# A causal convolution and a maxout feed-forward layer on one core: convolution groups of five blocks, an early exp table, and tiles at multiples of 256 bytes

## The chip, the core and the metric

The kernel runs on one core of a Trainium2 chip. The metric is the device time of one execution in microseconds (us). The kernel before takes 454.34 us, the median of three runs (454.12 to 455.48). Engines are named as the profile names them: PE is TensorE (matmuls; PEld its weight loads), DVE is VectorE, ACT is ScalarE, POOL is GpSimd, SP is the engine that issues most DMAs.

## The reference

The input `x` is 8 x 4160 x 192 in float32. The first layer is a causal convolution of 7 taps along the sequence; each of 8 heads has its own 7 weights (a softmax) for its 24 channels. The second layer is a maxout of three products with 768 columns, followed by a product back to 192 columns.

```python
w = np.exp(weight - np.max(weight, axis=-1, keepdims=True))
w = w / (np.sum(w, axis=-1, keepdims=True) + 1e-09)
x_pad = np.concatenate([np.zeros((B, K - 1, D)), x], axis=1)
y = np.einsum('hk,bskhg->bshg', w, unfold(x_pad)).reshape(B * S, D)
h = np.maximum(np.maximum(y @ w1, y @ w2), y @ w3)
out = h @ w_out
```

## The kernel before

**Blocks.** The 33280 rows are cut into 65 blocks of 512 tokens. Blocks 0 to 3 go through a dense convolution (`conv_dense`); block 4 stands alone, blocks 5 to 12 go in pairs, and blocks 13 to 64 in groups of four (`pairs`, lines 172 to 175; `place(t)` gives a block's group, its position in it and the group's size). The blocks of a group are convolved together.

**The way of a block.** SP loads its rows of x in float32 into a tile `xf`, one of three that take turns in the steady part (`load_x`). POOL casts it to float16 into its place in the group's tile `x16` (`cast_x`, line 194). TensorE convolves (`conv`, line 357): the 8 heads times 4 token strips times 2 halves are 64 matmuls for a group, each 39 rows by 32 columns of weights from the tile `band`, which holds the softmax weights as a banded matrix; the moving side has 48 columns for each block of the group, so 192 for a group of four. Groups of four are convolved in two halves of 4 heads (32 matmuls), in two successive blocks. A half writes four PSUM tiles G: two from the pool `psw`, one from `psp`, one from `psq` (`WPWQ`). `evac` (line 397) casts them to float16 in `ys`, two on ACT (those of `psw`) and two on DVE (those of `psp` and `psq`). `turn` (line 411) has SP transpose `ys` into the tile `yp` by DMA, two blocks at a time, and `double` (line 420) has POOL copy `yp` across the two halves of the partitions.

**The feed-forward layer.** For block t and column tile j (6 of 128 columns), `l1` forms two products lp and lq in PSUM, with weights that are differences with w3 (`wd`); `top` takes the relu of lp on ACT (line 490) and the larger of it and lq on DVE (line 491), which gives `h`. What the differences leave out is added back in the second product by the small matrices `m16`. `st2` forms the output product po of block t-1 (line 567), ACT copies one half, DVE adds the other (lines 574, 575), SP stores the result.

**The order.** All instructions stand in the program's own order (`manual_schedule`). PE is used as two halves of 64 rows, two lanes, that run side by side; `mm` queues matmuls by lane, `emit` gives them out so that the lanes' columns stay level, and `meet` empties both lanes. A convolution needs the whole array, so `meet` stands before it. In the loop over t (line 747) a block whose entry in `convs_at` names a group (`late`) does that group's convolution after column tile 1. For a group that begins at u these are blocks u-4 and u-3; `turn(u)` follows in u-3, and the third and fourth blocks' `turn` in u-2. The tables `casts` and `loads` say which block's cast and load is issued in which block t.

**PSUM buffers.** `psp` and `psq` have two buffers each. lp and lq of successive column tiles alternate between them, and a convolution takes one of each in between: lp and lq of column tile 3 of a late block go into the buffers that the two DVE casts of G have just emptied.

**The start.** ACT's queue loads the conv weights `wk`; the softmax on ACT and DVE (lines 265 to 274), 38 small matmuls that spread it (line 283) and casts on ACT and DVE (line 287) make `band`. Beside it SP loads x and the weights of the second layer into `ws` and `w3s`, POOL and DVE form `wd` from them (line 302), and PE runs matmuls on zeros (`keep_warm`, line 252) between its first tasks. ACT also writes zeros into parts of later `xf` tiles (line 137). The first product of block 0 with weights is `l1_dense` (line 526).

Of the kernel before, what the change touches and what calls it, by code (L numbers as in the profile page):

```python
# [10 lines left out]
FP32 = mybir.dt.float32  # L11
FP16 = mybir.dt.float16
AXX = mybir.AxisListType.X
# [15 lines left out]
def kernel(  # L29
# [71 lines left out]
    x16q = ctx.enter_context(tc.tile_pool(name="x16q", bufs=2))  # L101
    ysp = ctx.enter_context(tc.tile_pool(name="ysp", bufs=2))
    ydp = ctx.enter_context(tc.tile_pool(name="ydp", bufs=4))
    ypp = ctx.enter_context(tc.tile_pool(name="ypp", bufs=4))
    rp = ctx.enter_context(tc.tile_pool(name="rp", bufs=4))
    hp = ctx.enter_context(tc.tile_pool(name="hp", bufs=2))
    tp = ctx.enter_context(tc.tile_pool(name="tp", bufs=2))
# [3 lines left out]
    psq = ctx.enter_context(tc.tile_pool(name="psq", bufs=2, space=bass.MemoryType.PSUM))  # L111
    psw = ctx.enter_context(tc.tile_pool(name="psw", bufs=4, space=bass.MemoryType.PSUM))

    QUADS = 13
    assert (NB - QUADS) % 4 == 0
    xin, xbuf, XBUF, loaded = {}, [], 7, set()

    def get_x(t):
# [52 lines left out]

    pairs = {NDENSE: (NDENSE, 0, 1)}
    for t in range(NDENSE + 1, NB):
        u = (t - NDENSE - 1) % 2 if t < QUADS else (t - QUADS) % 4
        pairs[t] = (t - u, u, 2 if t < QUADS else 4)

    def place(t):
        return pairs.get(t, (t, 0, 0))
# [3 lines left out]
    def cast_x(t):  # L182
        if not 0 <= t < NB:
            return
        xf, p0, _ = xin.pop(t)
        t0, u, nu = place(t)
        if u == 0:
            pool = x16q if nu == 4 else x16p
            x16s[t0] = pool.tile([P, NHEAD, 4, nu, 2, GRP], FP16, tag="x16", name=f"x16_{t0}")
        if p0:  # L190
            nc.gpsimd.memset(xf[0:p0, 0, :], 0.0)
        K = HALF + KR
        for r in range(2):
            nc.gpsimd.tensor_copy(out=x16s[t0][0:K, :, :, u, r, :].rearrange("p h j c -> p j h c"),  # L194
                                  in_=xf[0:K, 4 * r:4 * r + 4, :].rearrange("p j (h c) -> p j h c", c=GRP))
# [18 lines left out]

    ws = const.tile([P, NC, DFF], FP32)
    w3s = const.tile([P, 2, DFF], FP32)
    PW = 2 * P

    def load_wa(f):
# [4 lines left out]
        for st, lo, n, wsrc in ((w3s, 0, 1, moe_w3), (ws, 0, 2, moe_w1), (ws, HALF, 2, moe_w2)):  # L226
            nc.sync.dma_start(out=st[lo:lo + HALF, n, f], in_=wsrc[P:D, f])

    wk = const.tile([NHEAD, KW], FP32)
    nc.scalar.dma_start(out=wk[:], in_=weight)  # L230
    wos = const.tile([P, NJ, D], FP32)
    load_x(0)
    load_wa(slice(0, PW))
# [21 lines left out]

    line = const.tile([NHEAD, WIN + 31], FP16)
    nc.vector.memset(line[:], 0.0)
    for v in range(2):  # L260
        nc.vector.memset(xz[0][v][:], 0.0)
    band = const.tile([P, NHEAD, BAND_W], FP16)
    nc.vector.memset(band[:], 0.0)
    keep_warm(5, psp, "p")
    wexp = const.tile([NHEAD, KW + 1], FP32)
    nc.vector.memset(wexp[:], 1e-9)
    wneg = const.tile([NHEAD, 1], FP32)
    nc.vector.reduce_max(out=wneg[:], in_=wk[:], axis=AXX, negate=True)
    nc.scalar.activation(out=wexp[:, 0:KW], in_=wk[:], func=AF.Exp, bias=wneg[:])  # L269
    wrec = const.tile([NHEAD, 1], FP32)  # L270
    nc.vector.reduce_sum(out=wrec[:], in_=wexp[:], axis=AXX)
    nc.vector.reciprocal(out=wrec[:], in_=wrec[:])
    zero_x(4)
# [21 lines left out]
    wd = const.tile([P, NC + 1, DFF], FP16)  # L295
    w3t = const.tile([P, NJ, 2 * P], FP16)
    wo = const.tile([P, NJ, D], FP16)
    m16 = const.tile([P, 3, D], FP16)

    def make_wd(n, j0, j1, eng=nc.vector):  # L300
        f = slice(P * j0, P * j1)
# [99 lines left out]
    def turn(t, vs=(0,)):  # L401


        nu = place(t)[2]
        for v in vs:
            n = min(nu, 2)
            yp = ypp.tile([P, 2, 2, n, NC, P], FP16, tag="yp", name=f"yp_{t + v}")
            for u in range(n):
                dense[t + v + u] = yp
            for i in range(2):  # L410
                nc.sync.dma_start_transpose(out=yp[:, 0, i, :, :, :].rearrange("p u k n -> p (u k) n"),
                                            in_=slots[t][:, i, v:v + n, :, :].rearrange("p u r d -> p (u r d)"))
# [10 lines left out]
    def spot(t, i, c, r):  # L423

        _, u, nu = place(t)
        u, nu = u % 2, min(nu, 2)
        f = NC * (r % 2) + c
        return (((f % 2 != i) * 2 + r // 2) * nu + u) * NC + f // 2

# [299 lines left out]

    convs_at = {2: 4, 3: 5, 4: 7}  # L730
    convs_at.update({t - 3: t for t in range(9, QUADS, 2)})
    convs_at.update({t - 4 + i: t for t in range(QUADS, NB, 4) for i in range(2)})
    casts = {4: 9}
    for t in range(5, NB):
        casts[t] = min(NB - 1, casts[t - 1] + (2 if t in (6, 7, 8) else 1))
    loads = {t: min(NB - 1, casts.get(t + 1, 0) + (t < 7 or t > 9)) for t in range(4, NB)}
    loads.update({2: 9, 3: 10})

    def load_on(t):
        for v in range(loads[t - 1] + 1, loads[t] + 1):  # L740
            if v not in loaded:
                load_x(v)
# [4 lines left out]
    for t in range(2, NB):  # L747
        u = convs_at.get(t, NB)
        late = t > 2 and u < NB
        if t in (3, 4):  # L750
            double(t + 1)
        if t > 3:
            for v in range(casts.get(t - 1, 8) + 1, casts[t] + 1):
                cast_x(v)
        l1(t, 0)
        if t == 2:
            first_rest()
        elif t == 3:
            cast_x(8)
            nc.gpsimd.tensor_copy(out=m16[0:HALF, 2, :], in_=m16[HALF:P, 0, :])  # L760
            nc.gpsimd.tensor_copy(out=m16[HALF:P, 2, :], in_=m16[HALF:P, 1, :])
        if t > 3 and not late:
            op(lambda t=t: (store(t - 2, 0, 4, (nc.sync,)),
                            turn(t + 2, (2,)) if place(t + 2)[1:] == (0, 4) else None, load_on(t)))
        else:
            op(lambda t=t: store(t - 2, 0, 4, (nc.sync,)))
        cuts = ROOM if late else EVEN
        st2(t - 1, (cuts[0], cuts[0]))
        for j in range(1, NJ):
            l1(t, j)  # L770
            if late and j == 1:
                st2(t - 1, (cuts[0] + OWN + AHEAD, cuts[0] + OWN))
                meet()
                quad, second = u >= QUADS, u < QUADS or t == u - 3
                conv(u, WPWQ, range(4 * second, 4 * second + 4) if quad else range(NHEAD))
                for i in (0, 2):
                    evac(u, i)
                for i in (1, 3):
                    evac(u, i, nc.vector.tensor_copy)
                if second:  # L780
                    turn(u)
                load_on(t)
            if t == 2 and j == 1:
                meet()
                conv_dense(3, (ACT, DVE))
                zero_x(1, NQ, NR, nc.vector)
                cross(3, GP)
                load_x(8)
                cast_x(6)
            elif t == 2 and j == 3:  # L790
                meet()
                conv(u, WW)
                evac(u, 0)
                evac(u, 1, nc.vector.tensor_copy)
                turn(4)
                load_x(9)
                cast_x(7)
            st2(t - 1, (cuts[j], cuts[j]))
            if j == 1 and t > 4 and t + 2 in pairs and pairs[t + 2][1] % 2 == 0:
                double(t + 2)  # L800
            if t == NB - 1 and j == 3:
                op(lambda: store(NB - 2, 0, 2, (nc.sync,)))
        if t == NB - 1:
            op(lambda: store(NB - 2, 2, 4, (nc.sync,)))
# [29 lines left out]
```

## Time and profile before

| What | us |
|---|---|
| median of three runs | 454.34 |
| the profiled execution | 454.51 |
| its span (first to last instruction) | 452.7 |
| PE busy | 446.8 |
| DVE busy | 356.5 |
| ACT busy | 320.0 |
| POOL busy | 202.9 |
| idle time of POOL ended by x loads / by transposes | 93.0 / 75.9 |
| mean of a DVE cast of G, 128x384 | 0.550 |
| mean of an ACT cast of G, 128x384 | 0.482 |

The profile is of one execution. Its page gives each engine's busy time; "the chain that ended last" follows the work back from the last instruction, at each step to what released it, so it tells which engine's work sets the time in each stretch. "The waits" list, for an engine, whom it sat idle for. The timeline shows rows of equal instructions with the first one's start, their time, and in brackets the idle time ahead of them. A busy engine that is not on the chain can become faster without any effect on the end.

### The profile page before, as it was taken

The numbers are of one execution on the slowest core, as the hardware profiler recorded it, in microseconds if no ns is written. First come the engines' busy times: TensorE is split into PE (matmuls) and PEld (weight loads), VectorE is DVE, ScalarE is ACT, GpSimd is POOL, SyncE is SP. The second block draws the span as 40 slices with busy tenths as digits, with TensorE's granted clock in tenths as the row PEclk, the third lists the DMA queues.
The fourth block names the chain that finished last, engine by engine and source line by source line (L and its number), as shares of the span: only waits on it lengthen the run. The fifth ranks groups of instructions, "written<-read, shape, count | busy, mean of one in ns | idle before, by whom it ended". The sixth has DMA issues, their size and how long they took to land.

```text
span 452.7 us, 18493 instructions
## 1 busy us (share of the span) xinstructions
PE 446.8 (99%) x7702; PEld 412.6 (91%) x7702; DVE 356.5 (79%) x617; ACT 320.0 (71%) x604; POOL 202.9 (45%) x226
## 2 busy tenths in 40 slices
PE   7999999999999999999999999999999999999997
PEld 3569999999999999999999999999999999999996
DVE  7768778878878787887878788887878788787775
ACT  7767767767777676777767777776767777776664
POOL 2864836556454534645263464535346452505000
PEclk9999999999999999999999999999999999999999
DMA  7969997596875869587685949657594776535223
GB/s 205 231 178 166 199 205 195 146 206 180 169 180 147 168 129 207 138 176 185 118 190 141 210 117 184 177 136 186 133 206 124 178 189 118 117 89 104 59 72 106
DMA packets 127987, 72.03 MB, mean 159 GB/s; under 512 B 52064, under 2 KB 127711, under 8 KB 127903
## 3 DMA queue, kind: packets, MB, share of 16 engines
q1 hardware_dynamic: 127743, 70.75, 68.3%
q8 instruction: 60, 0.98, 1.0%
q14 instruction: 24, 0.20, 0.1%
q10 hardware_dynamic: 160, 0.10, 0.1%
HBM read 33.28 MB, written 25.56 MB: 130 GB/s over the span
## 4 chain that ended last, share of the span: by engine, by line
PE 97%; ACT 1%; DMA 0%; DVE 0%; issue 0%; ACTq 0%
PE po L567 36%; PE lq L503 31%; PE lp L503 22%; PE G L357 3%; PE lw L526 1%; PE lp L526 1%; PE D L378 1%; PE po L625 0%; PE po L598 0%; DMA wk<-in_weight_dram 0%; PE lq L526 0%; ACT xf L137 0%; ACT band L287 0%; ACT L269 0%; PE pm L337 0%; PE band L283 0%
## 5 line engine op out<-in xcount | busy, mean ns | idle before, releaser
L491 DVE TENSOR_TENSOR h<-r,lq 128x512 f16<-128x512 f16 x384 | 263.0, 686 | 85.1 <-ACT r L490 77.3
L567 PE MATMUL po<-wo,h 64*128 64x192 f16 x3024 | 329.8, 243 | 0.0
L490 ACT ACTIVATE r<-lp 128x512 f16<-128x512 f32 x384 | 229.0, 597 | 114.3 <-PE lp L503 100.8
L503 PE MATMUL lp<-yp,wd 64*128 64x512 f16 x1098 | 295.6, 376 | 0.0
L503 PE MATMUL lq<-yp,wd 64*128 64x512 f16 x1098 | 295.5, 376 | 0.0
L567 PEld LDWEIGHTS <-h 64*128 64x128 f16 x3024 | 240.9, 94 | 6.3 <-issue 4.1
L503 PEld LDWEIGHTS <-wd 64*128 64x128 f16 x2268 | 177.7, 94 | 10.6 <-issue 0.2
L194 POOL CAST x<-xf 103x768 f16<-103x768 f32 x122 | 97.5, 827 | 106.6 <-DMA xf<-in_x_dram 93.0
L567 PE MATMUL po<-m,yp 64*128 64x192 f16 x720 | 141.0, 243 | 0.0
L420 POOL COPY yp<-yp 64x1536 f16<-64x1536 f16 (+1 forms) x62 | 89.6, 1445 | 96.2 <-DMA yp<-ys 75.9
L575 DVE TENSOR_TENSOR o<-a,po 128x384 f32<-128x384 f32 x126 | 69.0, 547 | 0.0
L567 PEld LDWEIGHTS <-yp 64*128 64x128 f16 x720 | 66.3, 94 | 0.5
L574 ACT COPY a<-po 128x384 f32<-128x384 f32 x126 | 59.5, 472 | 0.0
L397 ACT CAST ys<-G 128x384 f16<-128x384 f32 x61 | 26.3, 482 | 9.5 <-PE G L357 9.4
L397 DVE CAST ys<-G 128x384 f16<-128x384 f32 x61 | 31.0, 550 | 0.0
L357 PE MATMUL G<-x,band 39*32 39x192 f16 (+2 forms) x1152 | 17.3, 234 | 0.0
L357 PEld LDWEIGHTS <-band 39*32 39x32 f16 x1152 | 10.7, 91 | 5.2 <-issue 4.7
L503 PE MATMUL lp<-yd,wd 64*128 64x512 f16 x36 | 9.7, 376 | 0.0
L503 PE MATMUL lq<-yd,wd 64*128 64x512 f16 x36 | 9.7, 376 | 0.0
L526 PEld LDWEIGHTS <-wd 128*128 128x128 f16 (+1 forms) x48 | 3.2, 98 | 5.7 <-issue 2.4
L211 POOL CAST xz<-xf 112x160 f16<-112x160 f32 (+2 forms) x15 | 4.1, 319 | 7.7 <-DMA xf<-in_x_dram 7.7
L378 PEld LDWEIGHTS <-xz 112*32 112x32 f16 x320 | 4.6, 107 | 2.7 <-issue 1.0
(74 smaller groups left out, 98.2 us busy)
## 6 DMA issues: line engine op xcount, KB each, us to landing
xf<-in_x_dram SPq DMA_DIRECT2D x113, 234.0 KB
out_dram<-o SPq DMA_DIRECT2D x62, 384.0 KB
xf<-in_x_dram SPq DMA_DIRECT2D x7, 204.8 KB
xf<-in_x_dram SPq DMA_DIRECT2D x3, 420.0 KB
ws<-in_moe_w_dram SPq DMA_DIRECT2D x8, 128.0 KB
yp<-ys SPq DMA_TRANSPOSE x62
out_dram<-o SPq DMA_DIRECT2D x5, 192.0 KB
wos<-in_moe_w_out_dram SPq DMA_DIRECT2D x1, 576.0 KB
```

What stands on the lines that cost most here:

```text
L194: nc.gpsimd.tensor_copy(out=x16s[t0][0:K, :, :, u, r, :].rearrange("p h j c -> p j h c"), in_=xf[0:K, 4 * r:4 * r + 4, :].rearrange("p j ( ...
L357: nc.tensor.matmul(G[2 * (k // per) + i][TOK * j:TOK * (j + 1), k % per, :], lhsT=band[row, h, HALF * i + LAP:HALF * i + KR], rhs=x16s[t0] ...
L378: nc.tensor.matmul(ps[32 * g:32 * g + 32, lo:hi], lhsT=xz[t][v][0:rlen, q, 32 * s:32 * s + 32], rhs=band[0:rlen, h, cc:cc + hi - lo], star ...
L397: copy(out=slots[t][:, i % 2, :, :, GRP * h0:GRP * (h0 + per)].rearrange("p u r (h c) -> p h (u r) c", c=GRP), in_=G[i][:].rearrange("p h ...
L420: nc.gpsimd.tensor_copy(out=yp[HALF * i:HALF * (i + 1), 1, :, :, :, :].rearrange("p i u k n -> p (i u k n)"), in_=yp[HALF * (1 - i):HALF * ...
L490: nc.scalar.activation(out=r[:], in_=ps[0][:], func=AF.Relu)
L491: nc.vector.tensor_max(out=hs[t][:, j, :], in0=r[:], in1=ps[1][:])
L503: nc.tensor.matmul(ps[i][:], lhsT=w_of(i, c, j), rhs=y_all(t, i, c), start=(n == 0), stop=(n == NC - 1))
L526: nc.tensor.matmul(open_ps[t, j, i][:], lhsT=a, rhs=b, start=(t, j, i) not in begun, stop=(t, j, i) in begun)
L567: nc.tensor.matmul(ps[b0, i][:, s % 2, :], lhsT=a, rhs=b, start=first, stop=last)
L574: nc.scalar.copy(out=a[:], in_=ps[s - 1, 0][:])
L575: nc.vector.tensor_add(out=outs[t][:, s - 1:s + 1, :], in0=a[:], in1=ps[s - 1, 1][:])
```

## The change

- **Groups.** Blocks 25 to 64 are convolved in 8 groups of five; blocks 13 to 24 stay in 3 groups of four. The matmuls of a group of five move 240 columns. `turn` takes the blocks of a group as two, two and one; the fifth block's transposes are issued in block u-1 after the store. From block 16 on every cast, and with it every load, comes one block earlier. The pool of `yp` gets a fifth buffer, `x16` and `ys` grow to the size of five.
- **Weights in a pool.** `ws` and `w3s` are no longer tiles of their own: they are views of one buffer of the pool of `x16`, which a later group uses again.
- **Exp table.** A one-element exp on a zero tile stands on ACT right after the issue of the load of `wk`, so the table of exp is loaded there. The maximum of `wk` and the real exp come before the memset of `band` in DVE's and ACT's order.
- **Addresses.** A filler tile and rounded sizes of the small tiles put every tile that a DMA reads or writes at a multiple of 256 bytes within its partition.

```diff
-    ypp = ctx.enter_context(tc.tile_pool(name="ypp", bufs=4))
+    ypp = ctx.enter_context(tc.tile_pool(name="ypp", bufs=5))
...
-    QUADS = 13
-    assert (NB - QUADS) % 4 == 0
+    QUADS, QUINTS = 13, 25
+    assert (QUINTS - QUADS) % 4 == 0 and (NB - QUINTS) % 5 == 0
+    LINE = 256
+    SMALL = LINE // 4
+    const.tile([P, LINE // 4], FP16, name="edge")
...
-        u = (t - NDENSE - 1) % 2 if t < QUADS else (t - QUADS) % 4
-        pairs[t] = (t - u, u, 2 if t < QUADS else 4)
+        first_, nu = (NDENSE + 1, 2) if t < QUADS else (QUADS, 4) if t < QUINTS else (QUINTS, 5)
+        u = (t - first_) % nu
+        pairs[t] = (t - u, u, nu)
...
-            pool = x16q if nu == 4 else x16p
-            x16s[t0] = pool.tile([P, NHEAD, 4, nu, 2, GRP], FP16, tag="x16", name=f"x16_{t0}")
+            pool = x16q if nu >= 4 else x16p
+            x16 = pool.tile([P, NHEAD * 4 * 2 * GRP * (5 if nu >= 4 else nu)], FP16, tag="x16", name=f"x16_{t0}")
+            x16s[t0] = x16[:, 0:NHEAD * 4 * 2 * GRP * nu].rearrange("p (h j u r c) -> p h j u r c", h=NHEAD, j=4, u=nu, r=2)
...
-    ws = const.tile([P, NC, DFF], FP32)
-    w3s = const.tile([P, 2, DFF], FP32)
+    wall = x16q.tile([P, NHEAD * 4 * 2 * GRP * 5], FP16, tag="x16", name="wall")
+    wall = wall[:].bitcast(FP32).rearrange("p (n f) -> p n f", f=DFF)
+    ws, w3s = wall[:, 0:NC, :], wall[:, NC:NC + 2, :]
...
-    wk = const.tile([NHEAD, KW], FP32)
+    wk = const.tile([NHEAD, SMALL], FP32, name="wk")[:, 0:KW]
     nc.scalar.dma_start(out=wk[:], in_=weight)
+    warm = const.tile([1, SMALL], FP32, name="warm")[:, 0:1]
+    nc.vector.memset(warm[:], 0.0)
+    nc.scalar.activation(out=warm[:], in_=warm[:], func=AF.Exp)
...
-    band = const.tile([P, NHEAD, BAND_W], FP16)
+    wexp = const.tile([NHEAD, SMALL], FP32, name="wexp")[:, 0:KW + 1]
+    nc.vector.memset(wexp[:], 1e-9)
+    wneg = const.tile([NHEAD, SMALL], FP32, name="wneg")[:, 0:1]
+    nc.vector.reduce_max(out=wneg[:], in_=wk[:], axis=AXX, negate=True)
+    nc.scalar.activation(out=wexp[:, 0:KW], in_=wk[:], func=AF.Exp, bias=wneg[:])
+    bands = const.tile([P, LINE // 2 * ceil(NHEAD * BAND_W * 2 / LINE)], FP16, name="band")
+    band = bands[:, 0:NHEAD * BAND_W].rearrange("p (h w) -> p h w", w=BAND_W)
     nc.vector.memset(band[:], 0.0)
     keep_warm(5, psp, "p")
-    wexp = const.tile([NHEAD, KW + 1], FP32)
-    nc.vector.memset(wexp[:], 1e-9)
-    wneg = const.tile([NHEAD, 1], FP32)
-    nc.vector.reduce_max(out=wneg[:], in_=wk[:], axis=AXX, negate=True)
-    nc.scalar.activation(out=wexp[:, 0:KW], in_=wk[:], func=AF.Exp, bias=wneg[:])
-    wrec = const.tile([NHEAD, 1], FP32)
+    wrec = const.tile([NHEAD, SMALL], FP32, name="wrec")[:, 0:1]
...
-            n = min(nu, 2)
+            n = min(nu - v, 2)
...
-    convs_at.update({t - 4 + i: t for t in range(QUADS, NB, 4) for i in range(2)})
+    convs_at.update({t - 4 + i: t for t in (*range(QUADS, QUINTS, 4), *range(QUINTS, NB, 5)) for i in range(2)})
...
-        casts[t] = min(NB - 1, casts[t - 1] + (2 if t in (6, 7, 8) else 1))
+        casts[t] = min(NB - 1, casts[t - 1] + (2 if t in (6, 7, 8, 16) else 1))
...
-                            turn(t + 2, (2,)) if place(t + 2)[1:] == (0, 4) else None, load_on(t)))
+                            turn(t + 2, (2,)) if place(t + 2)[1:] in ((0, 4), (0, 5)) else None,
+                            turn(t + 1, (4,)) if place(t + 1)[1:] == (0, 5) else None, load_on(t)))
```

## The prediction

> **What bounds the kernel now.** I read the busy times first, then the chain that ended last, then the waits of TensorE, and last two stretches of the timeline: the start, and one convolution in the steady part. The busy times, TensorE's part of the waits, and the chain in order of time (columns: start, duration, what):
>
> ```profile
> span 452.7 us, 18493 instructions
> PE 446.8 (99%) x7702; PEld 412.6 (91%) x7702; DVE 356.5 (79%) x617; ACT 320.0 (71%) x604; POOL 202.9 (45%) x226
> ...
> PE band L283 <- DVE line L274: 1.3, 1, 1.3
> PE idle L252 <- DVE idle L247: 1.2, 1, 1.2
> ...
> 0.75 1.69 DMA wk<-in_weight_dram
> 2.50 1.28 ACT L269
> 7.14 1.48 ACT xf L137
> 9.27 0.58 PE lp L526
> 104.87 0.45 PE G L357 x32
> 111.80 0.46 PE G L357 x32
> 131.44 0.45 PE G L357 x32
> ```
>
> From 9.27 us on the chain is TensorE alone, and TensorE waits for no one in the steady part. So only two things can move the end: TensorE's own work, and the chain ahead of 9.27. Nothing that POOL, SP or the DMAs gain counts, unless they become late. The three convolution lines give prices. From 104.87 to 111.80 lies one block with one half convolution, 6.93; from there to 131.44 lie three blocks with one, 19.64. So a plain block takes (19.64 - 6.93) / 2 = 6.355 and a half convolution adds 6.93 - 6.355 = 0.575. Two half convolutions serve a group of four.
>
> The same convolution at closer range, the timeline of VectorE and TensorE (an idle time before the row stands in brackets):
>
> ```profile
> 104.96 0.69 DVE L491 TENSOR_TENSOR h<-r,lq 128x512 f16<-128x512 f16 x1 [0.37 <-ACT r L490]
> 105.56 1.01 DVE L397 CAST ys<-G 128x384 f16<-128x384 f32 x2
> 106.83 0.69 DVE L491 TENSOR_TENSOR h<-r,lq 128x512 f16<-128x512 f16 x1 [0.25 <-ACT r L490]
> ...
> 106.33 0.38 PE L503 MATMUL lp<-yp,wd 64*128 64x512 f16 x1
> 106.67 0.38 PE L503 MATMUL lq<-yp,wd 64*128 64x512 f16 x1
> ```
>
> The convolution takes one of the two buffers of each of the pools psp and psq. The two VectorE casts empty them, and the lp and lq of column tile 3 are next in those buffers: in the built program both carry a wait for VectorE. The second cast ends at 105.56 + 1.01 = 106.57; lq starts at 106.67. A wait on VectorE takes about 0.05 from its end to TensorE's start (line's end 4.73, band's start 4.78), so the margin is about 0.05 us, the smallest that I find in the loop.
>
> **The change, part by part.**
>
> *Fewer, wider convolutions.* Blocks 25 to 64 are 10 groups of four before and 8 of five after: 20 half convolutions become 16. Without growth that is 4 x 0.575 = 2.30 saved.
>
> Each half convolution has 32 matmuls on 8 places of the array, four rounds; in the trace the rounds start 0.083 us apart, which for 192 columns is 80 ns of streaming at 512 columns in 0.213 us (the lp matmuls follow each other by 0.216) and 3 ns more. With 240 columns a round is 0.103. So 4 x 0.020 = 0.08 more for each, 16 x 0.08 = 1.28. If nothing waits, the part saves 2.30 - 1.28 = 1.02.
>
> The casts of G grow from 384 to 480 columns. VectorE's rows: 384 columns 0.550 (cast of G), 512 columns 0.692 (cast of D), which is 1.1 ns a column; from start to start 0.467 for 384 columns and 0.60 for 512. So 480 columns take 0.65, and the next can start after 0.567. The first starts where it does now, since it queues behind h of column tile 1 and not behind the convolution. So the second ends 0.10 + 0.10 = 0.20 later, at 106.77, and lets lq go at 106.82. TensorE is ready for it at 106.67 + 0.08, less 0.01 that it waits for the h of tile 1 now and will not: 106.74. That is a wait of about 0.08 where there is none, on the lane of lq. The lp lane goes on (its next matmul is due 0.09 after lq, 106.76 now), but both lanes must be drained before the next convolution, and in the trace the lq lane's last matmul ends no earlier than the other's. So the 0.08 is paid each time: 16 x (0.08 + 0.01 lost slack) = 1.3. I take +0.3 for the whole part (1.28 + 1.3 - 2.30). Its bounds: -1.0 with no wait, and +0.7 if each cast takes 0.015 more than I interpolate (twice 0.015 by 16 is 0.48; 0.3 + 0.48 rounded down). I stand near the upper end because both prices come from rows of the same engine on both sides of 480.
>
> ScalarE's two casts grow too (0.482 at 384 columns, r 0.597 at 512: 0.57). They end at about 106.3 instead of 106.09; the r that follows starts at 106.20 and its lp comes 0.08 later, so it loses nothing, and the psw buffers are asked for at 106.51 at the earliest. Nothing.
>
> *Exp table early.* ScalarE's queue issues the load of wk until 1.33 (0.75 + 0.58); then the table's 1.28 ends at 2.61 instead of 3.78, and the one-element exp at about 0.30 later. The real exp then runs 2.91 to 3.22 instead of 3.80 to 4.11: 0.89 earlier. The bounds: nothing, if the table takes as much longer at that place, and 1.18, set by wk's landing at 2.44, the maximum (0.14) and the exp (0.31). What is moved ahead on VectorE is a memset of one element (0.05 to 0.1) and wexp's memset; band's memset (0.51) now follows the maximum, which waits for wk, and ends at about 3.1, ahead of exp's end. The sums, the reciprocal, line, the band matmuls, the band casts and ScalarE's zero fill (1.48) all follow one another and move by 0.89; xf of block 0 has landed at 4.40, ahead of the casts at 4.76. So the first dense product goes from 9.27 to 8.38.
>
> From there on other things are late next:
>
> ```profile
> 9.39 0.86 POOL L211 CAST xz<-xf 112x160 f16<-112x160 f32 x3 [7.72 <-DMA xf<-in_x_dram]
> 13.40 2.79 POOL L302 TENSOR_TENSOR wd<-ws,w3s 128x256 f16<-128x256 f32 x4 [1.40 <-DMA ws<-in_moe_w_dram]
> ...
> 10.08 0.63 PE L526 MATMUL lp<-yd,wd 128*128 128x512 f16 x1
> 10.51 0.53 PE L526 MATMUL lq<-yd,wd 128*128 128x512 f16 x1
> 10.96 1.11 PE L378 MATMUL D<-band,xz 112*32 112x103 f16 x80
> 15.05 0.39 PE L526 MATMUL lp<-yd,wd 64*128 64x512 f16 x1
> ```
>
> POOL's two waits for DMAs do not move. Block 1's dense convolution can begin at about 9.95, after two of the three casts. The lp of 15.05 needs the first of the four subtractions, done at 14.13: with 0.05 for the wait it can come 0.87 earlier and no more. And TensorE is at half speed until about 10.8: the dense matmuls start 0.43 apart, later ones 0.216. If the speed rises at the same moment as now, the part of the convolution that lies at half speed grows by 0.65, which costs 0.33: gain 0.56. I take 0.75 of the range 0.56 to 0.87.
>
> The Trainium skill's page "TensorE: Matmul & The Clock Gate", section "What's actually happening", says that the clock is halved until one whole free-running window of about 3.4 us was busy. By that rule the idle 1.26 us ahead of the band matmuls is what holds the clock back here, it shrinks to 0.37, and the full clock could come a window earlier; the gain would then be the 0.87, and the total 0.1 better. No run here shows it yet.
>
> *Addresses.* In the built programs the tiles of x that start at 160 and 128 past a multiple of 256 move to 0. In the trace's packet records the 768-byte packets take 36 ns at the median in the first 5 us, when only tiles at 160 are filled, and 36 ns later, when two tiles of three already stand at 0. I take nothing; bounds are 0.2 either way, a tenth of the 2.3 us in which block 1's data come in.
>
> The Trainium skill's "DMA: Bandwidth & Descriptors", section "How a descriptor splits into AXI transactions", would have a 768-byte read that starts 128 past the line cost 28 beats in place of 24. That concerns the output stores, whose end no one here waits for.
>
> *Moved and added work, off the path.* For 40 blocks SP issues 48 pairs of transposes in place of 40 (16 x 3 matrices instead of 6 in 8 of the pairs); a pair holds SP for 2.55 to 3.4 us, the extra ones less, and SP now waits 179.7 us for output tiles. Behind the new transposes stand the x loads for blocks cast two blocks later. POOL's copies of yp come to the same sum (4 of 1.45 and 2 of 0.85 for five blocks, against 4 of 1.45 for four). Every cast from block 24 on is done one block earlier, x two casts (1.6 each) in block 16; POOL's waits of 93.0 us for x and 75.9 us for yp cover it. If the cover were gone, a convolution would wait up to a cast, 1.6. The fifth yp buffer keeps each transposed tile's reuse behind blocks already finished.
>
> **Sum.** -0.75 at the start, +0.3 in the loop: -0.45. The profiled execution took 454.51, which is 0.17 above the median 454.34; so 454.06 against it, 453.9 against the median.
>
> **Rivals.** (A) The casts fit and lq does not wait. For it: the margin is of the size of the error. Against: two rows bracket the price. 454.34 - 0.75 - 1.02 = 452.6. (B) The start gives nothing, because the table's load or the two DMAs take up the gain: 454.34 + 0.3 = 454.6. For it: POOL's 7.72 us behind the x load. (C) Slower: the wait of lq for the cast is longer than computed and holds the lp lane as well. From 0.11 instead of 0.08 + 0.01 the loop eats the start's gain (16 x (0.08 + 0.11) - 2.30 = 0.75); at 0.20 the time is 454.34 - 0.75 + 16 x 0.28 - 2.30 = 455.8. Against: nothing else is queued on VectorE between the two.
>
> **How the numbers follow.** My forecast 0.52 (its own range 453.3 to 454.6), A 0.27, B 0.12, C 0.09. This kernel's measurement can tell about 0.3%, 1.36 us: faster means under 452.98, slower over 455.70. A lies mostly under it, with a little of the forecast: 0.27. C is about half over it, with a little of B: 0.08. Within: 0.65. The range goes from A's 452.6 less 0.2 to 455.0.
>
> **What would show it.** Right: exp's table load starts near 1.3 and the first dense lp near 8.4; half convolutions are spaced so that each adds 0.73 to 0.74 to a block; TensorE's waits list lq behind the cast of G, some 0.08 each, 16 times; VectorE's cast of 128x480 takes 0.65. Wrong: the cast of 480 columns under 0.6, lq starting 0.97 after the lq of tile 2 as now, or TensorE waiting for x, yp or ys anywhere.

## The result, and the profile after

| | before | after |
|---|---|---|
| median of 18 runs each, us | 454.27 | 453.41 |
| lowest and highest | 453.58, 455.49 | 452.74, 454.40 |
| profiled execution | 454.51 | 453.45 |
| its span | 452.7 | 451.7 |

The ratio after to before is 0.9974, with a 95% interval of 0.9964 to 0.9985: 0.26% faster. This is inside the 0.3% that the prediction calls no change, though the interval leaves out 1. The forecast was 453.9 with a range of 452.4 to 455.0. The total came out close to it; three terms of the sum (the loop, the early exp, the addresses) did not, as the rest of this document shows.

The busy times, and the row of VectorE's casts of G, from the page of the changed kernel:

```profile
span 451.7 us, 18257 instructions
PE 447.2 (99%) x7574; PEld 410.0 (91%) x7574; DVE 357.0 (79%) x610; ACT 319.2 (71%) x597; POOL 203.8 (45%) x234
...
L407 DVE CAST ys<-G 128x480 f16<-128x480 f32 (+1 forms) x53 | 30.2, 610 | 0.0
```

The mean of 610 ns mixes the shapes; the casts of 480 columns alone take 646 to 652 in the trace's records (the single instructions and packets that the views are made of). The waits of TensorE (engine, line, whom it waited for, sum, times, longest):

```profile
PE idle L261 <- DVE idle L256: 1.2, 1, 1.2
PE lq L513 <- DVE yd L399: 0.2, 1, 0.2
PE band L293 <- DVE line L284: 0.2, 1, 0.2
```

The list of before had a third row, which the prediction did not use:

```profile
PE D L378 <- issue: 0.4, 1, 0.4
```

Here "issue" means that TensorE waited for no engine and no data that the profile shows. Against that list, the wait for the softmax has gone from 1.3 to 0.2, the 0.4 put down to "issue" is absent, and one wait of an lq for a DVE copy of yd is new. No wait for x, yp or ys is there. The wait of lq for the cast of G is not listed either, although it exists: while one lane waits the other works, and the list counts only time in which all of TensorE is idle.

The chain that ended last, in order of time (start, duration, what):

```profile
8.22 0.58 PE lp L536
...
10.08 1.45 PE D L388 x58
...
25.26 0.37 PE lq L513
...
30.66 0.60 PE G L367 x64
...
104.25 0.46 PE G L367 x32
...
111.18 0.45 PE G L367 x32
...
130.83 0.46 PE G L367 x32
...
157.40 0.53 PE G L367 x31
...
164.48 0.53 PE G L367 x32
...
190.57 0.54 PE G L367 x32
```

**The loop.** The groups of four keep their spacings of before (104.25 to 111.18 is 6.93, on to 130.83 is 19.65). In a group of five the second half follows the first by 7.08, which is a block of 6.355 and 0.725; the next group's first half follows by 26.09, which is four blocks and 0.67. So the sixteen halves cost 8 x 0.725 + 8 x 0.67 = 11.16, where twenty cost 20 x 0.575 = 11.5: a gain of 0.34. Taken whole, the stretch from block 21's half convolution (the first for block 25) to the end is 294.75 us in the records of before and 294.34 in those after, 0.42 less; the last half, which no convolution follows, has a part in the difference between 0.42 and 0.34.

**The start.** The first dense lp begins at 8.22 instead of 9.27, 1.05 earlier. At the first convolution of block 4 the chain of before stands at 31.25 and this one at 30.66, 0.59 earlier. It looks as if half of the early gain had come through. The timeline between the two shows that none of it did in these two executions. Before, POOL, DVE and PE (start, duration, what, and in brackets the idle time ahead):

```profile
23.98 0.69 DVE L389 COPY yd<-yd 64x512 f16<-64x512 f16 x2 [2.37 <-ACT yd L383]
...
24.72 1.60 POOL L194 CAST x<-xf 103x768 f16<-103x768 f32 x2 [0.52 <-DMA xf<-in_x_dram]
...
25.55 0.50 PE L606 MATMUL po<-m,yd 128*128 128x192 f16 x4
...
27.31 0.97 PE L378 MATMUL D<-band,xz 112*32 112x103 f16 x67
28.68 0.34 PE L378 MATMUL D<-band,xz 112*32 112x103 f16 x13 [0.40 <-issue]
```

The same stretch after:

```profile
23.44 1.76 DVE L399 COPY yd<-yd 64x512 f16<-64x512 f16 x2 [2.37 <-ACT yd L393]
...
24.23 1.66 POOL L199 CAST x<-xf 103x768 f16<-103x768 f32 x2 [0.15 <-DMA xf<-in_x_dram]
...
25.26 0.37 PE L513 MATMUL lq<-yd,wd 64*128 64x512 f16 x1 [0.19 <-DVE yd L399]
25.56 0.50 PE L616 MATMUL po<-m,yd 128*128 128x192 f16 x4
...
27.33 1.10 PE L388 MATMUL D<-band,xz 112*32 112x103 f16 x80
```

The two DVE copies come 0.54 earlier and take 1.76 instead of 0.69, so they end later than before (25.20 against 24.67), and an lq waits for them. Before, they fell mostly into POOL's idle 0.52; after, a POOL cast runs beside each. At 25.56 both kernels are level (25.55 before), at 27.33 again (27.31). What parts them afterwards is the gap of block 3's dense convolution: before has an idle 0.40 between its 67th and 68th matmul, the changed kernel runs through. The ends of matmuls are modelled; from start to start the step is 0.61 before and 0.01 after, which is all of the 0.59. The early exp had no part in it in these two executions.

### The profile page after: what moved, and what is told of

It is laid out like the page before. It is cut to its first block, busy times and chain, and to the rows that moved or that the text cites. A ratio compares the mean times of both kernels' runs of the same rounds, so it can differ in the third digit from the quotient of the medians.

```text
span 451.7 us, 18257 instructions
## 1 busy us (share of the span) xinstructions
PE 447.2 (99%) x7574; PEld 410.0 (91%) x7574; DVE 357.0 (79%) x610; ACT 319.2 (71%) x597; POOL 203.8 (45%) x234
## 3 DMA queue, kind: packets, MB, share of 16 engines
HBM read 33.28 MB, written 25.56 MB: 130 GB/s over the span
## 4 chain that ended last, share of the span: by engine, by line
PE 97%; DVE 1%; ACT 0%; issue 0%; ACTq 0%
PE po L577 36%; PE lq L513 32%; PE lp L513 22%; PE G L367 3%; PE lw L536 1%; PE lp L536 1%; PE D L388 1%; PE po L635 0%; PE po L608 0%; PE lq L536 0%; DVE yd L399 0%; DVE xz L216 0%; DVE xz L286 0%; ACT L239 0%; DVE wd L312 0%
## 5 line engine op out<-in xcount | busy, mean ns | idle before, releaser
L513 PEld LDWEIGHTS <-wd 64*128 64x128 f16 x2268 | 181.7, 94 | 15.0 <-issue 0.2
L199 POOL CAST x<-xf 103x768 f16<-103x768 f32 x122 | 97.2, 825 | 113.4 <-DMA xf<-in_x_dram 98.3
L430 POOL COPY yp<-yp 64x1536 f16<-64x1536 f16 (+1 forms) x70 | 90.9, 1298 | 85.4 <-DMA yp<-ys 53.7
L407 ACT CAST ys<-G 128x480 f16<-128x480 f32 (+1 forms) x53 | 25.4, 530 | 9.5 <-PE G L367 9.5
L407 DVE CAST ys<-G 128x480 f16<-128x480 f32 (+1 forms) x53 | 30.2, 610 | 0.0
L367 PE MATMUL G<-x,band 39*32 39x240 f16 (+3 forms) x1024 | 16.5, 242 | 0.0
```

What stands on the lines that cost most here:

```text
L367: nc.tensor.matmul(G[2 * (k // per) + i][TOK * j:TOK * (j + 1), k % per, :], lhsT=band[row, h, HALF * i + LAP:HALF * i + KR], rhs=x16s[t0] ...
L407: copy(out=slots[t][:, i % 2, :, :, GRP * h0:GRP * (h0 + per)].rearrange("p u r (h c) -> p h (u r) c", c=GRP), in_=G[i][:].rearrange("p h ...
L430: nc.gpsimd.tensor_copy(out=yp[HALF * i:HALF * (i + 1), 1, :, :, :, :].rearrange("p i u k n -> p (i u k n)"), in_=yp[HALF * (1 - i):HALF * ...
L513: nc.tensor.matmul(ps[i][:], lhsT=w_of(i, c, j), rhs=y_all(t, i, c), start=(n == 0), stop=(n == NC - 1))
```

## The experiments

All ratios are against the kernel before, timed on the same chip as the experiment, with a 95% interval.

### The early exp alone, twice

In the first version the one element is a tile of its own:

```diff
     wk = const.tile([NHEAD, KW], FP32)
     nc.scalar.dma_start(out=wk[:], in_=weight)
+    warm = const.tile([1, 8], FP32, name="warm")
+    nc.vector.memset(warm[:, 0:1], 0.0)
+    nc.scalar.activation(out=warm[:, 0:1], in_=warm[:, 0:1], func=AF.Exp)
...
-    band = const.tile([P, NHEAD, BAND_W], FP16)
-    nc.vector.memset(band[:], 0.0)
-    keep_warm(5, psp, "p")
...
+    band = const.tile([P, NHEAD, BAND_W], FP16)
+    nc.vector.memset(band[:], 0.0)
+    keep_warm(5, psp, "p")
```

> The kernel before with the early exp alone (table loaded behind the issue of wk, maximum and exp ahead of band's memset); groups, addresses and buffers as before. Theory: the two profiles differ by 0.62 us at the first convolution of a group of four in block 21 and by 0.4 us more in the loop, so the early exp is worth about 0.6: 454.27 - 0.6 = 453.7, and the half convolutions keep their spacing of 6.93 and 19.64 us. Rival 1 (the start gives nothing lasting, since in the profile after the gain of 0.54 was used up at 25.3 us by the slow copies of yd): 454.2 to 454.4. Rival 2 (the start gives the whole gain): 453.4.

Measured: 455.66 against 454.35, ratio 1.0058 (1.0029 to 1.0087): 0.6% slower. The new tile had moved every later tile by 32 bytes, so two things were changed and not one. In the records the 768-byte packets took 50.3 ns in the mean, against 46.3 before. Its runs spread up to 461.24, and the profiled one, with 454.93, is one of the faster, so the profile need not show what the others lost. TensorE's waits in it:

```profile
PE po L601 <- POOL wo L701: 0.7, 1, 0.7
PE D L381 <- issue: 0.3, 1, 0.3
```

The first is new: POOL got the weights of the output product late. So the early exp was tried again with every address left where it was, its element put into four spare bytes behind `wk`:

```diff
-    wk = const.tile([NHEAD, KW], FP32)
+    wkw = const.tile([NHEAD, KW + 1], FP32, name="wk")
+    wk, warm = wkw[:, 0:KW], wkw[0:1, KW:KW + 1]
     nc.scalar.dma_start(out=wk[:], in_=weight)
+    nc.vector.memset(warm[:], 0.0)
+    nc.scalar.activation(out=warm[:], in_=warm[:], func=AF.Exp)
```

> The early exp alone once more, now with every tile at its old address (the warm-up element sits in the 4 spare bytes behind wk). The earlier run moved all later tiles by 32 bytes, and its DMA packets were longer (768 bytes: 50.3 ns mean against 46.3). Theory (the loss of that run came from the addresses; the early exp itself is worth little, because the start is caught up at other waits by 31 us): 454.1 to 454.4, first dense product near 8.2 us, first convolution of a group (block 4) within 0.3 of 31.25. Rival 1 (the early exp by itself makes things collide and costs): 455 or more. Rival 2 (it is worth 0.6 as predicted): 453.7.

Measured: 454.57 against 454.59, ratio 0.9995 (0.9981 to 1.0009). The first dense lp starts at 8.22 as in the changed kernel, and the medians show nothing of it at the end. TensorE's waits show what took it up in this execution:

```profile
PE D L381 <- issue: 0.8, 1, 0.8
PE D L381 <- POOL xz L211: 0.3, 1, 0.3
PE band L286 <- DVE line L277: 0.2, 1, 0.2
```

Block 1's convolution now waits 0.3 for its data, which POOL could cast from 9.97 on (from 9.39 in the profile of before), since the DMA landed later, and the gap of block 3 is 0.8 where before had 0.4. By the medians the early exp is worth nothing (0.02). The interval, -0.86 to +0.41, does not quite exclude a gain of 0.75; that it is near 0 rests on this run, on the next one and on the timelines together.

### Groups of five with the exp late

The changed kernel without the early exp:

```diff
-    warm = const.tile([1, SMALL], FP32, name="warm")[:, 0:1]
-    nc.vector.memset(warm[:], 0.0)
-    nc.scalar.activation(out=warm[:], in_=warm[:], func=AF.Exp)
...
+    bands = const.tile([P, LINE // 2 * ceil(NHEAD * BAND_W * 2 / LINE)], FP16, name="band")
+    band = bands[:, 0:NHEAD * BAND_W].rearrange("p (h w) -> p h w", w=BAND_W)
+    nc.vector.memset(band[:], 0.0)
+    keep_warm(5, psp, "p")
     wexp = const.tile([NHEAD, SMALL], FP32, name="wexp")[:, 0:KW + 1]
```

> The changed kernel with the exp put back to its old place: groups of five and the new addresses alone. Theory: 16 half convolutions that add 0.725 (first of a group) and 0.67 (second) against 20 that add 0.57: 8 x 1.395 - 20 x 0.5715 = -0.27, so 454.27 - 0.3 = 454.0, with the first dense product back at about 9.2 us. Prediction's number for the loop (+0.3): 454.6. Rival (the loop gives the whole gain): 453.4.

Measured: 453.62 against 454.35, ratio 0.9984 (0.9973 to 0.9994). The spacings of the halves are 7.09 and 26.08, block 4's convolution starts at 30.65, the same as with the early exp (30.66). Leaving the exp late costs nothing that the intervals can tell. The stretch from block 21's half convolution to the end is 294.47 here.

### The addresses alone

The changed kernel with the exp late, and with groups of four to the end:

```diff
-    QUADS, QUINTS = 13, 25
+    QUADS, QUINTS = 13, NB
...
-        casts[t] = min(NB - 1, casts[t - 1] + (2 if t in (6, 7, 8, 16) else 1))
+        casts[t] = min(NB - 1, casts[t - 1] + (2 if t in (6, 7, 8) else 1))
```

> Groups of four to the end and the exp at its old place: of the change only the addresses, the weights' place in the pool and the fifth yp buffer are left. Theory (TensorE's gap of 0.40 us at 28.3, which the profile puts down to nothing it shows, is a late fetch of its instructions, and it is absent with aligned tiles as in the two profiles with groups of five): 453.7, no gap over 0.1 us on TensorE between 12 and 450 us. Rival (the gap is chance, the addresses give nothing): 454.3.

Measured: 453.87 against 454.59, ratio 0.9981 (0.9967 to 0.9996). What is left of the change here is the addresses, with the place of the weights in a pool and the fifth buffer of yp, which were not taken apart. These bring 0.86 by the ratio (0.19% of 454.3), between 0.2 and 1.5. By the times alone groups of five add nothing to that (0.9984 with them in the run above, 0.9981 here, intervals of more than 0.1% either way); the 0.3 to 0.4 of the loop stands in the records, where the stretch from block 21's half convolution to the end is 294.72 here. TensorE's waits are those of before without the 0.4 of "issue":

```profile
PE idle L258 <- DVE idle L253: 1.2, 1, 1.2
PE band L290 <- DVE line L281: 1.0, 1, 1.0
```

### The addresses taken away again

The changed kernel with a smaller filler, so that all of the tiles that DMAs touch lie together 192 bytes past a multiple of 256 (with `LINE // 2` in the same place, the second run, they lie 128 past):

```diff
-    const.tile([P, LINE // 4], FP16, name="edge")
+    const.tile([P, LINE // 8], FP16, name="edge")
```

> The changed kernel with the filler tile at 64 bytes in place of 128, so that every tile that a DMA touches stands 192 bytes past a multiple of 256; nothing else differs. Theory (addresses give nothing): the time of the changed kernel, 453.4, within 0.3, with x landing at the same time, 9.3 to 9.4 us for block 1. Rival (addresses are part of the gain): 453.7 or more, and a larger share of the DMA engines.

> The changed kernel with a filler tile of 256 bytes, so that every tile that a DMA touches stands 128 past a multiple of 256. Theory (half lines are as good as whole ones, since before most tiles stood at 0 or 128 and its 768-byte packets had the same mean, 46.3 against 46.0 ns, while 192 past gave 52.6): 453.4, packets at 46 ns. Rival (only multiples of 256 are good): 454.5 or more as with 192, packets at 50 ns or more.

Measured: at 192 past, 454.71 against 454.35, ratio 1.0014 (0.9995 to 1.0033); at 128 past, 454.23 against 454.59, ratio 0.9986 (0.9971 to 1.0001). At 192 the whole gain of the change is gone, and the interval lies apart from that of the changed kernel (0.9964 to 0.9985) although nothing but the addresses differs; at 128 the middle of the interval lies between. The mean 768-byte packet took 52.5 ns at 192, 48.5 at 128, and 44.7 to 46.0 in the eight executions with multiples of 256. The waits in which the 192 case differs most:

```profile
PE D L388 <- issue: 0.9, 1, 0.9
PE G L367 <- issue: 0.8, 1, 0.8
```

These are not waits for slow transfers of x. They are put down to "issue"; more on them below. The case of 128 has such gaps of 0.6 and 0.4.

### The cross copies on POOL

If the DVE copies beside POOL's casts take up the early gain, they could be given to POOL, ahead of the cast that disturbs them:

```diff
+    cross(2, GP)
     cast_x(4)
-    cross(2)
```

> The changed kernel with block 2's two cross copies of yd on POOL ahead of its cast of block 4, instead of on VectorE beside it. In the profile after, the two VectorE copies took 0.79 and 0.96 us and ended with POOL's casts (24.23, 25.2); before they took 0.33 each in a gap of POOL. Theory (VectorE's float16 copy cannot run while POOL works, and this used up the start's gain): copies end at about 24.65, the lq that waited until 25.26 starts at 24.7, and the first convolution moves from 30.66 to about 30.1: 453.41 - 0.5 = 452.9. Rival (another wait, the next in line, takes it up before 31 us): 453.4.

Measured: 453.88 against 454.59, ratio 0.9977 (0.9959 to 0.9994), no better than the changed kernel. The timeline of POOL and PE in this kernel:

```profile
20.76 3.39 POOL L216 CAST xz<-xf 112x240 f16<-112x240 f32 x12 [1.53 <-DMA xf<-in_x_dram]
24.21 1.28 POOL L399 COPY yd<-yd 64x512 f16<-64x512 f16 x2
...
25.55 0.37 PE L513 MATMUL lq<-yd,wd 64*128 64x512 f16 x1 [0.19 <-POOL yd L399]
```

POOL itself is late in this execution, held by a load of x, and the lq waits as long for POOL (0.19) as it did for DVE. Moving the copies moved the wait from one engine to the other. The theory of 452.9 failed; what the start would gain with POOL on time was not shown.

### The changed kernel again

The changed kernel without an edit, on the chip of the last two experiments below:

> The changed kernel itself, on the chip of the next two: 453.4 if its first measurement stands; in its profile no gap on TensorE at 28 us (the 16 KB fetch of its instructions ends before 26.7), the halves of a group of five 7.08 apart.

Measured: 453.53 against 454.59, ratio 0.9982 (0.9971 to 0.9992). As expected, its profile has no gap at 28 us and halves 7.08 apart; from block 21's half convolution to the end it takes 294.34, as in the first profile.

### One matmul more or less before the lq that waits

`ROOM` is the running count of the output products (po) of the block before that are queued after each column tile of a late block; its third number stands ahead of tile 3, its fourth ahead of tile 4. One po more there gives the casts of G about 0.08 us more, one less takes as much away, in every late block, those of groups of four and of pairs too. The edit for one more (for one less the two numbers are 16 and 20):

```diff
-    ROOM = [5, 13, 17, 21, 26, 30]
+    ROOM = [5, 13, 18, 22, 26, 30]
```

> The changed kernel with one more output matmul on each lane between column tiles 2 and 3 of a late block (the cuts 17 and 21 become 18 and 22), so that the lq of tile 3 comes 0.083 us later by itself. Theory (that lq waits 0.084 us for the second VectorE cast in the first half of a group of five and 0.013 in the second, and both are paid at the next convolution): 8 x 0.097 = 0.78 less, 452.65; the spacing of the halves of a group falls from 7.08 to 7.00. Rival (the wait is absorbed anyway, or the cast's delay comes back at tile 4): 453.4, spacing unchanged.

> The kernel with one more output matmul on each lane ahead of column tile 3, again, on the same chip as the changed kernel: 0.5 to 0.8 under it (0.4 us less in the loop's first halves by 8 x 0.08 = 0.64 and 8 x 0.013 = 0.10 for the second ones by the theory that the wait for the cast is paid at the next convolution); the same as it by the rival that the wait is absorbed.

> The other way: one output matmul less on each lane ahead of column tile 3 (cuts 16 and 20), so that its lq is due 0.083 us earlier while the cast ends when it did. Theory: the wait of the first halves grows from 0.084 to 0.167 and their spacing from 7.08 to 7.16; in the second halves VectorE starts its casts earlier by the same amount, as it did already (0.683 instead of 0.755 after the convolution's start), and the wait stays near 0.01 to 0.02: 8 x 0.083 = 0.66 more than the changed kernel. Rival (absorbed): the same as the changed kernel.

Measured: one more, 452.62 against 454.35 on the first chip and 453.06 against 454.59 on the second; the ratio is 0.9959 both times (0.9943 to 0.9975, and 0.9945 to 0.9973). One less, on the second chip, 454.92, ratio 1.0004 (0.9992 to 1.0016). The chains of the two on the second chip, one more first:

```profile
158.51 0.54 PE G L367 x32
...
165.51 0.54 PE G L367 x32
...
191.59 0.54 PE G L367 x32
```

One less:

```profile
165.59 0.54 PE G L367 x32
...
191.76 0.53 PE G L367 x32
...
198.85 0.54 PE G L367 x32
```

With one more, halves stand 7.00 and 26.08 apart: a half adds 0.645 and 0.66, which is the price of 240 columns without any wait, 0.575 + 0.08. With one less they stand 26.17 and 7.09 apart: 0.75 and 0.735. Per group of five (two halves) this is 33.08, 33.17 in the changed kernel, and 33.26. So the room sets the wait, in steps of 0.08 and 0.09 a group, about 0.7 over eight groups. From block 21's half convolution to the end it is 293.68 with one more in both of its profiles, 294.34 in the changed kernel and 295.15 with one less. From the changed kernel's 453.53 on that chip the medians went by -0.47 and +1.39. With one less the groups of four wait too (their halves stand 6.96 apart, not 6.93). And the +1.39 holds more than the loop: its profile has a gap of 1.54 in block 3's convolution, where the changed kernel's had none (the one with one more has 0.75 there). With one po more the kernel is the fastest of this study. Its interval against the kernel before just overlaps that of the changed one (0.9971 to 0.9992); on the shared chip the means of its 10 runs and of the changed kernel's 12 differ by 0.75.

## Why the prediction was right in its total, and where its steps failed

| Step | predicted, us | measured, us | how |
|---|---|---|---|
| four half convolutions fewer | -2.30 | -2.30 | spacing of the groups of four unchanged |
| 240 columns, each of 16 | +0.08 | +0.08 | first lp after a half: 0.55 to 0.63 in the records |
| lq waits for the cast, each of 16 | +0.09 | +0.07 eight times, 0.01 eight times | spacings less 0.655 |
| loop, sum | +0.3 | -0.34 (-0.42 to the end) | spacings; block 21 to the end |
| early exp | -0.75 | about 0 (-0.86 to +0.41) | exp alone at the old addresses |
| addresses | 0 | about -0.5 in the profiles, -0.86 (-0.2 to -1.5) in the times | addresses alone |
| sum | -0.45 | -0.86 | medians |

The measured rows add up to -1.20, not to -0.86; the interval of the addresses alone is wider than that difference.

**The loop.** The mechanism was right: the cast of 480 columns takes 0.65 as interpolated, the two casts start 0.567 apart, and lq of tile 3 starts 0.05 after the second one's end. The failed step is "so the 0.08 is paid each time". It is paid at the first half of a group and hardly at the second. The sum was wrong as well: 16 x (0.08 + 0.01) is 1.44 and not 1.3, so the prediction's own terms give +0.42 for the loop. DVE and PE in the timeline of the changed kernel, the first half and then the second:

```profile
157.48 0.69 DVE L501 TENSOR_TENSOR h<-r,lq 128x512 f16<-128x512 f16 x1 [0.37 <-ACT r L500]
158.09 1.21 DVE L407 CAST ys<-G 128x480 f16<-128x480 f32 x2
...
158.29 0.38 PE L513 MATMUL lq<-yp,wd 64*128 64x512 f16 x1
...
159.35 0.37 PE L513 MATMUL lq<-yp,wd 64*128 64x512 f16 x1
...
164.49 0.69 DVE L501 TENSOR_TENSOR h<-r,lq 128x512 f16<-128x512 f16 x1 [0.29 <-ACT r L500]
165.09 1.22 DVE L407 CAST ys<-G 128x480 f16<-128x480 f32 x2
...
165.37 0.38 PE L513 MATMUL lq<-yp,wd 64*128 64x512 f16 x1
...
166.36 0.37 PE L513 MATMUL lq<-yp,wd 64*128 64x512 f16 x1
```

The lq rows are the first of tile 2 and the first of tile 3. They stand 1.06 apart in the first half and 0.99 in the second, where 0.97 is the distance without a wait, as before had it (the prediction shows the second of these rows):

```profile
105.70 0.37 PE L503 MATMUL lq<-yp,wd 64*128 64x512 f16 x1
106.67 0.38 PE L503 MATMUL lq<-yp,wd 64*128 64x512 f16 x1
```

In both halves of the changed kernel, tile 3 starts 0.05 after the end of the casts (159.30 and 166.31). But the casts begin earlier against the convolution in the second half: the convolutions' first matmuls start at 157.33 and 164.41, so h of tile 1, behind which the casts queue, begins 0.15 after the one and 0.08 after the other. The prediction took that lead to be fixed ("the first starts where it does now"). It is not. The wait of the first half leaves the lq lane 0.07 to 0.08 late. The records show it: the last po of each lane starts 0.17 to 0.18 ahead of the first half's convolution, but 0.17 ahead of the second half's in one lane and 0.25 in the other, which is done early. Both lanes are drained before the next convolution, which is therefore that much later against all that follows from the lp lane, and the relu and h of tile 1 follow from it: the relu ends 0.12 after the first convolution's start and 0.05 after the second's. So a wait at one half pays for most of the wait at the next, and then the lag is gone and the wait comes back.

The two ROOM kernels confirm it in their records. With one po more hardly any wait is left (lq of tile 3 starts 0.05 after the casts, and 1.06 after that of tile 2, where 1.06 is the distance with the extra po), and the casts begin 0.76 after the convolution in both halves. With one less the wait comes at every half, the lag never goes, and the casts begin 0.68 after it everywhere but in the first half of the first group of five (0.76). That kernel's 0.735 and 0.75 a half are near the 0.73 to 0.74 that the prediction gave to the changed kernel. Rival A, no wait, is nearly what the kernel with one po more has; rival C, a wait that holds the lp lane too, did not occur (lp of tile 3 starts 1.61 after the convolution in both halves).

**The start.** That the first dense lp comes earlier was right (8.22, predicted 8.38), and so was the loss to the clock: it rises at 10.76 after and at 10.79 before, which left 0.54 at 11.5, against 0.56 for that case. What failed is that a gain of 0.75 there was booked as kept to the end. The prediction looked for what is late next only up to 15 us (POOL's casts of xz, the subtractions). In the profile after, the wait that took the gain up lies at 25 us, in the copies on DVE. In seven other executions with the early exp, block 1's convolution waits 0.3 to 0.9 for xz and starts at 9.6 to 10.45. And in four of them (exp alone at the old addresses, 192 past, 128 past, one po less) some of the gain was still there at 25 us: the po row that starts at 25.55 before starts at 24.59 to 25.30. There the gap of block 3 took it up. At 192 past:

```profile
24.59 0.50 PE L616 MATMUL po<-m,yd 128*128 128x192 f16 x4
...
28.24 0.34 PE L388 MATMUL D<-band,xz 112*32 112x103 f16 x13 [0.92 <-issue]
```

So the early start meets three limits of their own time one after the other, and the prediction weighed only the first. Rival B, that the start gives nothing, was right about the start, and about one of its two causes in part: the DMA of x.

The Trainium skill's page "TensorE: Matmul & The Clock Gate", section "What's actually happening", has the clock's window free-running, so the rise may come up to a window earlier. It did not in the profile above; in the profile of the repeated run it rose at 8.40. Block 1's convolution could not start earlier by it, as this row of that run shows:

```profile
9.96 1.30 PE L388 MATMUL D<-band,xz 112*32 112x103 f16 x80 [0.64 <-POOL xz L216]
```

It starts at 9.96 with the early clock, where POOL's cast of its data sets it, and at 10.01 with the late one. But it then ran faster: the next lp starts at 11.19 with the early clock, at 11.47 with the late one and at 12.00 before, so at that point the gain was 0.81, near the 0.87 that the prediction worked out for an early clock. At the po row of 25.55 it was gone there as well (25.67).

**The addresses.** "I take nothing; bounds are 0.2 either way" failed: the kernel with the addresses alone (and the pool and the fifth buffer that came with them) gained 0.86, and only the weak end of that interval reaches 0.2. The reading was of medians of packets, in which the kernels do not differ (36 ns in both; the mean of all 768-byte packets is 46.3 before and 46.0 after). What differs between these two profiles is not the speed of the bulk of packets but the gap in block 3: 0.40 before, none after. That the addresses bring this about is argued, not shown. The Trainium skill's "DMA: Bandwidth & Descriptors", section "How a descriptor splits into AXI transactions", gives, for a read, 28 beats for 24 at 128 bytes past, an estimate of 17% more; the means here, over loads and stores together, were 5% more at 128 (48.5 ns) and 14% more at 192 (52.5) than the 46.0 of the changed kernel. The direction agrees, the size at 128 does not, and the measurement decides.

**ScalarE, and the work off the path.** Costed at nothing, and right: ACT's casts took 0.56, and TensorE waited for no x, yp or ys. POOL's cover for x stands at 98.3 us, that for yp shrank from 75.9 to 53.7.

So the total was near for a wrong reason: a gain of 0.75 that did not come, against a loss of 0.3 that was a gain of 0.34 and an effect of the addresses that was left out. That these errors partly cancelled was luck.

## What to carry to other kernels

A wait on one of two lanes that meet later is not paid at a fixed price each time: ask where the lag goes at the next meeting, and whether it gives the next wait a head start. An earlier start is kept only if no later transfer or engine with a time of its own sits between; walk the list of waits to the end of the ramp, not just past the first stage. Where a cast ends a few hundredths too late for the matmul that needs its buffer, one independent matmul queued ahead of it took the wait away here. An experiment that adds a tile must keep the other tiles' addresses or it measures two things.

## What the runs showed of the hardware

**TensorE stalls behind its instruction fetch.** The gap in block 3 always falls after the 67th of the 80 matmuls and is put down to "issue". In the DMA records a packet of 16384 bytes of kind "instruction" (queue 8) ends a little before. Where there was a gap of 0.06 or more, the next matmul began 1.36 to 1.58 us after that packet's end, in eight of eight executions: before 27.10 and 28.68, with one po more 27.41 and 28.93, with one less 27.42 and 28.98. Where there was none, the packet had ended by 24.87 to 26.46. The stops put down to "issue" elsewhere fit too: at 71.92 (192 past), 72.00 (one po more, second chip) and 33.35 (128 past) TensorE went on 1.55, 1.54 and 1.49 after the end of such a packet. The gap was 0.34 to 0.92 in all five executions with other addresses; with the tiles at multiples of 256 it was 0 in five, 0.06 in one, and 0.75 and 1.54 in two. So it was rarer with these addresses, in few executions, and they do not end it. That slower packets on the same engines delay the fetch is argued from this, not shown; what makes the fetch start at 23.7 in one execution and at 26.4 in another stays open. These are single profiled executions of each kernel.

**A copy on DVE waits for the cast on POOL.** The view of the tile yd, its copies on DVE (shortest, median and longest in ns, then the starts), before:

```profile
L389 DVE COPY yd<-yd x2: 287/330/372, 24.0 to 24.4; 64x512 f16<-64x512 f16 x2
```

And after:

```profile
L399 DVE COPY yd<-yd x2: 785/868/950, 23.4 to 24.3; 64x512 f16<-64x512 f16 x2
```

In the records a copy with no POOL cast beside it takes 0.287 to 0.289. One that begins while a cast runs on POOL ends 0.14 after that cast's end, whenever it began, unless its own 0.29 takes longer; one that begins before the cast keeps its 0.29 (128 past: the copy at 23.35, the cast at 23.37, 0.289): after, the casts end at 24.08 and 25.06 and the copies at 24.23 and 25.21; before, 24.21 and 24.35 for the first, and the second, with POOL idle, took 0.287. The same 0.14 stands in the profiles of nine of the experiments. So a copy of 0.29 took up to 0.95, which is what ate the early start in the profile after. The Trainium skill's "GPSIMD Engine Reference", section "Specifications", says that GpSimd shares its SBUF interfaces with VectorE and that they contend for instructions in a mode that uses two ports or with two SBUF inputs. The copies agree with such contention; that they run in that mode is shown by no run here. h, which takes r from SBUF and lq from PSUM, took 0.68 to 0.69 both beside a POOL cast and without one.

**The exp table's load costs the same earlier.** It took 1.28 at either place. After the change it runs beside the DMA of `wk` (1.35 to 2.63, where it was 2.50 to 3.79); the time that it freed did not reach the end here.
